# Who makes the small parts: lo parts moved to GpSimd, signs folded into ScalarE's scaling, and the first chunk's k and q turned on TensorE

## The chip, the core and the metric

The kernel runs on one core of a Trainium2 chip. The metric is the time of one execution on the device, in microseconds (us); the median of several runs counts. The engines are named as the profile names them: PE is TensorE (PEld its weight loads), DVE is VectorE, ACT is ScalarE, POOL is GpSimd, SP is SyncE, which only issues DMAs here. Each engine works through a queue of its own in order.

## What is computed

Attention in which a query sees only the keys of its own hash bucket, then a feed-forward block with ELU:

```python
batch, n_heads, seq, head_dim = (4, 8, 768, 64)      # proj: 64 x 6
q_bits = (np.einsum('bhsd,dk->bhsk', q, proj) > 0)   # k_bits in the same way
mask = q_bucket[:, :, :, None] == k_bucket[:, :, None, :]   # buckets: the six bits as a number
scores = np.where(mask, scale * np.matmul(q, k.transpose(0, 1, 3, 2)), -1000000000.0)
attn = softmax(scores)
x = np.matmul(attn, v)            # heads side by side: 3072 tokens x 512
h = x @ w_in                      # w_in: 512 x 2048, float64
g = np.where(h > 0.0, h, np.exp(np.minimum(h, 0.0)) - 1.0)
out = (g @ w_out).astype(np.float32)   # w_out: 2048 x 512, float64
```

## The kernel before

**Two fp16 numbers for one.** Each operand of a matmul is a pair: hi is the scaled value rounded to fp16, lo the rest. ScalarE makes hi (`scaled`, L143), VectorE makes lo (`rest`, L152) as `x * s - hi` in one instruction. Both are helpers, so many different tiles carry these two lines. The table `ENGINES` says which engine takes which kind, before and after all weights are decoded ("A", "V", "G" for ScalarE, VectorE, GpSimd).

**The work in order.** Batch 0 to 3, two chunks each of half the queries; a chunk has four pairs of heads. A pair's k (`prep_k`) and q (`prep_q`) are scaled by a power of two, split (`split`, tiles `natk`, `nat1q`, `nat2q`), turned from tokens on partitions to features on partitions by DMA transposes on SP's queue (L328, L371, L372, tiles `K1`, `O1`, `O2`), and projected: TensorE makes the hash sums, VectorE turns them to plus or minus bits (`bits`, L291), and small DMAs (L295) lay these as further rows under `K2` and `O2`, so that the scores' second matmul adds the mask. The scores (L508) go through VectorE (L520, maximum), ScalarE's exponential (L536), a split into `hl`, a DMA transpose of it (L551) and the product with V (`attend`, L559). V is split once a batch (`prep_v`, `vhl`).

**The weights** arrive as float64. `wload` (L456) brings 512 KB at a time on SP's queue into one of four staging places (three named `U`, one in `W`); `wdecode` makes float32 of it: ScalarE scales the high word (`w_mul`), VectorE shifts (L468), joins the low word (L469) and sets the sign (L479); TensorE sums magnitudes with a matrix of ones (L472) for the common scale (`wscale`, tiles `w0s` and `w1s` for the two matrices). `wsplit` then makes hi and lo of each of the 32 pieces. A piece's pair is written where the piece before it was read: place d takes the pair whose source is place d + 1.

**The feed-forward stream** (`moe_stream`) starts six slots after the first chunk's scores (a slot is one block of 128 queries of one head). `first` multiplies by w_in (L588), takes the exponential (L599, ScalarE), a GpSimd step (L602), a VectorE step (L603), and splits the result; `second` multiplies by w_out (L624). From there on the order of TensorE's queue is fixed by the program's order; elsewhere a scheduler sets each engine's order from dependences and its own estimates. When the steps of a pair's preparation are written is set by lists of slots: `PREP0` for the first chunk's four pairs (load, sums, split, project, counted before the pair's first slot), `VPREP` for V.

Of the kernel before, what the change touches and what calls it, by code (L numbers as in the profile page):

```python
# [7 lines left out]

# [25 lines left out]
PREP0 = (100, 12, 12, 6)  # L34
# [32 lines left out]
def lsh_attention_moe(  # L67
# [210 lines left out]

    def bits(o, ways, w, which):

        t = ps_a.tile([P, 512], F32, tag="av", name="z")[:, :w]
        quads = len(ways[0][1])
        for n, (x, moving) in enumerate(ways):
            for u, mv in enumerate(moving):
                rows = mv.shape[0]
                nc.tensor.matmul(  # L286
                    t[u * QD : (u + 1) * QD], pj["z"][:rows, x, :], mv, start=n == 0, stop=n == len(ways) - 1
                )
# [2 lines left out]
        nc.vector.tensor_scalar(  # L291
            zb[used], t[used], pj["thr"][used, which : which + 1], (MBIT, -MBIT)[which], ALU.is_gt, ALU.mult
        )
        for u in range(quads):
            d = nc.sync.dma_start(o[D : D + 2 * NB, u * w : (u + 1) * w], zb[u * QD : u * QD + 2 * NB])  # L295
        return d
# [3 lines left out]
    def prep_k(b, ps, sts, sgs):  # L300
        def load():
            with after(0, "first") if b == 0 and "first" in ks[0, 0] else nullcontext():
                for p, st, sg_ in zip(ps, sts, sgs):
                    st["kf"] = stg.tile([P, 2 * NC, D], F32, tag="k", name="kst", bufs=2) if sg_.kf is None else sg_.kf
                    nc.sync.dma_start(
                        st["kf"].rearrange("p (h c) d -> p h (c d)", h=2),
                        k[b, 2 * p : 2 * p + 2].rearrange("h (p c) d -> p h (c d)", c=NC),
                    )
# [13 lines left out]
        def split(st, sg_):  # L322
            s, nat = st["ksc"], sg_.k1
            scaled("n_hi", nat[:, :, :D], st["kf"], s)
            rest("n_lo", nat[:, :, D:], st["kf"], s, nat[:, :, :D])
# [2 lines left out]
            st["first"] = nc.sync.dma_start_transpose(st["K1"], flat(nat))  # L328
# [9 lines left out]
    def prep_q(b, c0, nc_, ps, ksts, sts, sgs):  # L338
        def load():
# [25 lines left out]
        def split(st, sg_):  # L365
# [5 lines left out]
            nc.sync.dma_start_transpose(st["O1"], flat(nat1))  # L371
# [88 lines left out]
    def wdecode(i):  # L460
# [6 lines left out]
        scaled("w_mul", d, hi.bitcast(F32), 2.0**-112)  # L467
        nc.vector.tensor_scalar(di, di, 3, None, ALU.logical_shift_left)  # L468
        nc.vector.scalar_tensor_tensor(di, lo, 29, di, ALU.logical_shift_right, ALU.bitwise_or)  # L469
# [2 lines left out]
        nc.tensor.matmul(  # L472
            wst["acc"], ones, d.bitcast(BF16).rearrange("p (n t) -> p n t", t=2)[:, :, 1],
            start=i == o * NSI, stop=i in (NSI - 1, NSI + NSO - 1),
        )
        if i in (NSI - 1, NSI + NSO - 1):
            nc.vector.tensor_reduce(wst["m2"][:, o : o + 1], wst["acc"], axis=AX.X, op=ALU.max)
        if engine("w_sgn") == "V":
            nc.vector.scalar_tensor_tensor(di, hi, -(2**31), di, ALU.bitwise_and, ALU.bitwise_or)  # L479
        else:  # L480
            sign = hi.bitcast(F32)
            nc.scalar.activation(sign, sign, AF.Sign)
            nc.gpsimd.tensor_tensor(d, d, sign, ALU.mult)
# [91 lines left out]
    def moe_stream(chunks):  # L575
# [4 lines left out]
        def first(c, f):  # L580
# [21 lines left out]
            nc.gpsimd.tensor_scalar(e, e, -1.0, 0.0, ALU.add, ALU.min)  # L602
            nc.vector.scalar_tensor_tensor(e, h, c["ch"], e, ALU.mult, ALU.max)  # L603
# [37 lines left out]
        for c in chunks:  # L641
            ch = small.tile([P, 1], F32, tag="ch", name="ch", bufs=2)
            sg = small.tile([P, 1], F32, tag="sgg", name="sgg", bufs=2)
# [316 lines left out]
```

## Time and profile before

| | |
|---|---|
| median of 3 runs (lowest to highest) | 937.68 us (936.27 to 938.84) |
| the profiled execution's own time, and its span | 935.8 us, 934.0 us |
| mean granted TensorE clock | 0.938 |
| instructions | 14523 |
| DMA bytes moved | 138.47 MB, 404586 packets |

The span is cut in stretches in the prediction. A row of a group reads: line, engine, operation, output <- inputs, partitions x elements, count, then busy time in all, mean time of one in ns, and the idle time of that engine just before these instructions with what ended it.

### The profile page before, as it was taken

What the parts mean: (1) busy time and instruction counts of PE and PEld (TensorE: products, weight loads), DVE (VectorE), ACT (ScalarE), POOL (GpSimd) and SP (SyncE); (2) the same over time, 40 slices, a digit from 0 to 9 for tenths busy, and PEclk for the clock granted to TensorE, in tenths of its full rate; (3) what the DMA queues carried; (4) which work ended last, traced back from release to release, by engine and by line L of the source; (5) the groups of instructions that cost most, each with busy time, mean ns of one, the idle gap of its engine ahead of it and who ended that gap; (6) DMA issues with size and microseconds to landing.
All of it is one profiled execution on the core that took longest, in us unless ns stands there. A gap on an engine that the chain in (4) does not pass through costs nothing.

```text
span 934.0 us, 14523 instructions
## 1 busy us (share of the span) xinstructions
PE 816.6 (87%) x4975; PEld 419.9 (45%) x4975; DVE 717.6 (77%) x1524; ACT 690.7 (74%) x1345; POOL 229.1 (25%) x177
## 2 busy tenths in 40 slices
PE   2445545889989999998989999999999999999996
PEld 0112212444545555554544555554455555555553
DVE  6798999888977877688868877888878778774332
ACT  4577886888978777788788777888878778774332
POOL 1000000222223232332323232333232223223432
PEclk9956656899999999999999999999999999999999
DMA  9999798759698677798988767795876767655000
GB/s 268 254 219 228 214 255 180 127 106 200 121 185 166 134 119 136 138 186 154 171 172 155 139 112 144 153 200 94 162 149 126 119 120 152 102 109 91 35 1 35
DMA packets 404586, 138.47 MB, mean 148 GB/s; under 512 B 380960, under 2 KB 398880, under 8 KB 404512
## 3 DMA queue, kind: packets, MB, share of 16 engines
q1 hardware_dynamic: 402432, 131.25, 70.6%
q0 software_dynamic: 1920, 6.29, 2.0%
q8 instruction: 39, 0.64, 0.3%
q14 instruction: 35, 0.29, 0.1%
q10 hardware_dynamic: 160, 0.00, 0.0%
HBM read 35.65 MB, written 6.29 MB: 45 GB/s over the span
## 4 chain that ended last, share of the span: by engine, by line
PE 49%; DVE 19%; DMA 14%; ACT 8%; issue 7%; POOL 2%; SPq 1%; ACTq 0%; POOLq 0%; DVEq 0%
PE o L624 17%; PE h L588 17%; PE s L508 7%; PE av L559 6%; DVE pt L520 4%; DMA K<-natk 4%; DVE hl L152 4%; ACT pt L536 3%; POOL U L602 2%; DMA O<-nat1q 2%; ACT hl L143 2%; DMA W<-in_moe_w_out_dram 2%; DMA out_dram<-W 1%; DVE vhl L152 1%; PE z L286 1%
## 5 line engine op out<-in xcount | busy, mean ns | idle before, releaser
L602 POOL TENSOR_SCALAR U<-U 128x384 f32<-128x384 f32 x128 | 212.9, 1663 | 670.4 <-ACT U L599 669.8
L588 PE MATMUL h<-x,W 128*128 128x384 f16 x1536 | 281.4, 327 | 4.1 <-DVE U L603 3.3
L624 PE MATMUL o<-W,U 128*128 128x512 f16 x1152 | 282.8, 382 | 1.6 <-DVE U L152 0.9
L152 DVE SCALAR_TENSOR_TENSOR hl<-pt,r,hl 128x768 f16<-128x768 f32 x192 | 191.5, 1019 | 20.0 <-ACT hl L143 19.9
L588 PEld LDWEIGHTS <-W 128*128 128x128 f16 x1536 | 147.8, 98 | 116.5 <-issue 15.8
L536 ACT ACTIVATE pt<-pt,nb,sg 128x768 f32<-128x768 f32 x192 | 195.4, 1018 | 2.3
L143 ACT ACTIVATE hl<-pt,r 128x768 f16<-128x768 f32 x192 | 168.4, 925 | 31.3 <-DVE r L546 30.3
L520 DVE TENSOR_SCALAR_CACHE_REDUCE pt<-s 128x768 f32<-128x768 f32 x177 | 167.9, 949 | 17.3 <-PE s L508 16.0
L508 PE MATMUL s<-K,O 128*128 128x384 f16 x708 | 152.7, 340 | 23.4 <-DVE pt L520 22.4
L624 PEld LDWEIGHTS <-U 128*128 128x128 f16 x1152 | 111.5, 98 | 122.9 <-issue 8.8
L603 DVE SCALAR_TENSOR_TENSOR U<-h,ch,U 128x384 f32<-128x384 f32 x128 | 78.4, 612 | 79.8 <-POOL U L602 79.8
L559 PE MATMUL av<-PT,vhl 128*64 128x384 f16 x1152 | 112.5, 347 | 20.3 <-DMA PT<-hl 6.0
L508 PEld LDWEIGHTS <-O 128*128 128x128 f16 (+1 forms) x768 | 75.0, 102 | 119.1 <-issue 48.7
L599 ACT ACTIVATE U<-h,ch 128x384 f32<-128x384 f32 x128 | 73.0, 570 | 59.1 <-PE h L588 58.6
L143 ACT ACTIVATE U<-U,sgg 128x384 f16<-128x384 f32 x128 | 77.3, 605 | 49.9 <-DVE U L603 49.9
L152 DVE SCALAR_TENSOR_TENSOR U<-U,sgg 128x384 f16<-128x384 f32 x128 | 79.1, 619 | 30.9 <-ACT U L143 30.9
L559 PEld LDWEIGHTS <-vhl 128*64 128x64 f16 x1152 | 71.5, 116 | 66.9 <-issue 12.9
L472 PE MATMUL acc<-W,ones 128*128 128x512 bf16 x32 | 16.8, 549 | 32.4 <-DVE W L469 32.4
L533 ACT ACTIVATE nb<-m,sg 128x2 f32<-128x2 f32 x96 | 27.6, 288 | 16.3 <-DVE pt L520 15.8
L536 ACT ACTIVATION_READ_ACCUMULATOR pt<-pt,nb,sg 128x1 f32 x192 | 36.0, 187 | 0.0
L291 DVE TENSOR_SCALAR zb<-z,pjt 64x384 f16<-64x384 f32 (+1 forms) x48 | 29.0, 604 | 1.4 <-PE z L286 1.1
L286 PEld LDWEIGHTS <-pjz 128*32 128x32 f16 (+1 forms) x320 | 9.3, 94 | 43.9 <-issue 29.8
(102 smaller groups left out, 539.2 us busy)
## 6 DMA issues: line engine op xcount, KB each, us to landing
U<-in_moe_w_in_dram SPq DMA_DIRECT2D x12, 512.0 KB
vf<-in_v_dram SPq DMA_DIRECT2D x16, 384.0 KB
U<-in_moe_w_out_dram SPq DMA_DIRECT2D x12, 512.0 KB
out_dram<-W POOLq DMA_DIRECT2D x24, 256.0 KB, 3.4
qst<-in_q_dram SPq DMA_DIRECT2D x30, 192.0 KB
kst<-in_k_dram SPq DMA_DIRECT2D x14, 384.0 KB
PT<-hl SPq DMA_TRANSPOSE x192
W<-in_moe_w_in_dram SPq DMA_DIRECT2D x4, 512.0 KB
```

The lines of the kernel that those rows point to most:

```text
L143: nc.scalar.activation(o, x, AF.Copy, scale=s)
L152: nc.vector.scalar_tensor_tensor(o, x, s, hi, ALU.mult, ALU.subtract)
L291: nc.vector.tensor_scalar(zb[used], t[used], pj["thr"][used, which : which + 1], (MBIT, -MBIT)[which], ALU.is_gt, ALU.mult)
L508: nc.tensor.matmul(s_tile[:, n, :HALF], st[o][:rows, at, :], kst[kk][:rows, j * NC + n * HC : j * NC + (n + 1) * HC, :].rearrange("p a b - ...
L520: top = nc.vector.tensor_scalar(pt.rearrange("p (n e) -> p n e", n=2), s_tile[:, :, :HALF], CLAMP, None, ALU.max, ALU.max, accum_out=duo[0 ...
L536: nc.scalar.activation(pt, pt, AF.Exp, bias=nb[:, n : n + 1], scale=st["sg"][:, 0:1], accum_out=sm[:, n : n + 1])
L559: nc.tensor.matmul(av[j * D : (j + 1) * D], vt[:, j, c, vx, :], PTs[j][:, :, px, c, :], start=n == 0, stop=n == last,)
L588: nc.tensor.matmul(h, WH[:, g * KT + t, wx, fc * P : (fc + 1) * P], c["xs"][t][:, xx, :], start=n == 0, stop=n == 3 * KT - 1,)
L599: nc.scalar.activation(e, h, AF.Exp, scale=c["ch"])
L602: nc.gpsimd.tensor_scalar(e, e, -1.0, 0.0, ALU.add, ALU.min)
L603: nc.vector.scalar_tensor_tensor(e, h, c["ch"], e, ALU.mult, ALU.max)
L624: nc.tensor.matmul(o[t][:, :DO], g16[:, gx, t * P : (t + 1) * P], WH[:, NSI + 1 + f, wx, :], start=f == 0 and i == 0, stop=f == NF - 1 and ...
```

## The change

Six things:

- **Weights' signs.** ScalarE's scaling of the high word becomes a Prelu with a slope that puts the sign where VectorE's two remaining steps want it; the step L479 goes. The scale of a matrix now comes from Gram products of its 128-column blocks (four small matmuls with the piece itself as both operands) in place of one matmul with ones.
- **Lo parts on GpSimd**: those of the weights always, those of V until all weights are decoded (batch 0). There `rest` is two instructions: a scaling in place (L153 of the changed kernel), then a difference (L154).
- **The first chunk's k and q** are turned by TensorE against an identity (`turned_by_pe`, L289), with ScalarE copying the result out of PSUM (L290). Their bits (`bits_beside`) are made on the partitions where they are needed, so that the small DMAs go.
- **The first chunk's steps are written at other slots**: all loads at the start, and sums, split and project of the four pairs at slots -50, 2, 7 and 12.
- **Loads that waited** for the first pair's turning and small DMAs (V's, and the weights' from the sixth on) now stand behind its first load.
- **The ELU** is kept divided by its scale: GpSimd makes `e * up + dn`, VectorE `min(max(h, 0), that)`, with four numbers a chunk instead of two.

The core of the diff:

```diff
-PREP0 = (100, 12, 12, 6)
+PREP0 = (-50, 2, 7, 12)
...
-    "v_lo": ("V", "V"),
-    "w_mul": ("A", "A"),
-    "w_sgn": ("V", "V"),
+    "v_lo": ("G", "V"),
     "w_hi": ("A", "A"),
-    "w_lo": ("V", "V"),
+    "w_lo": ("G", "G"),
...
+    def turned_by_pe(parts):
+        for o, nat in parts:
+            rows, n = o.shape[0], nat.shape[1]
+            for a in range(0, n, 8):
+                z = min(a + 8, n)
+                t = ps_h.tile([P, 512], F32, tag="h", name="turn").bitcast(F16).rearrange("p (n e) -> p n e", e=P)
+                for i in range(a, z):
+                    nc.tensor.transpose(t[:rows, i - a, :], nat[:, i, :rows], ident)
+                nc.scalar.activation(o[:, a:z, :], t[:rows, : z - a, :], AF.Copy)
+
+    def bits_beside(o, ways, which):
+        used = slice(D, D + 2 * NB)
+        for a in range(0, o.shape[1], 512):
+            w = min(512, o.shape[1] - a)
+            t = ps_h.tile([P, 512], F32, tag="h", name="zh")[:, :w]
+            for n, (x, mv) in enumerate(ways):
+                rows = mv.shape[0]
+                nc.tensor.matmul(
+                    t[D : D + QD], pj["z"][:rows, x, :], mv[:, a : a + w], start=n == 0, stop=n == len(ways) - 1
+                )
+            nc.vector.tensor_scalar(
+                o[used, a : a + w], t[used], pj["thr"][used, which : which + 1], (MBIT, -MBIT)[which], ALU.is_gt, ALU.mult
+            )
...
-            st["first"] = nc.sync.dma_start_transpose(st["K1"], flat(nat))
+            if early:
+                turned_by_pe([(st["K1"], nat)])
+                st["first"] = st["load"]
+            else:
+                st["first"] = nc.sync.dma_start_transpose(st["K1"], flat(nat))
...
+            if early:
+                bits_beside(k2, ((0, k1), (1, k1)), 0)
+                st["done"] = st["load"]
+                return
...
-        scaled("w_mul", d, hi.bitcast(F32), 2.0**-112)
+        nc.scalar.activation(d, hi.bitcast(F32), AF.Prelu, scale=2.0**-112, alpha=-(2.0**32))
         nc.vector.tensor_scalar(di, di, 3, None, ALU.logical_shift_left)
         nc.vector.scalar_tensor_tensor(di, lo, 29, di, ALU.logical_shift_right, ALU.bitwise_or)
...
-        nc.tensor.matmul(
-            wst["acc"], ones, d.bitcast(BF16).rearrange("p (n t) -> p n t", t=2)[:, :, 1],
-            start=i == o * NSI, stop=i in (NSI - 1, NSI + NSO - 1),
-        )
+        for u in range(FG):
+            x = top[:, u * P : (u + 1) * P]
+            nc.tensor.matmul(
+                wst["acc"][:, u * P : (u + 1) * P], x, x,
...
-        if engine("w_sgn") == "V":
-            nc.vector.scalar_tensor_tensor(di, hi, -(2**31), di, ALU.bitwise_and, ALU.bitwise_or)
...
-            nc.gpsimd.tensor_scalar(e, e, -1.0, 0.0, ALU.add, ALU.min)
-            nc.vector.scalar_tensor_tensor(e, h, c["ch"], e, ALU.mult, ALU.max)
+            nc.gpsimd.tensor_scalar(e, e, c["up"], c["dn"], ALU.mult, ALU.add)
+            nc.vector.scalar_tensor_tensor(e, h, 0.0, e, ALU.max, ALU.min)
```

The order of the queues shows three places. First GpSimd's queue up to the first ELU step (L602 before, L650 now). Before, only constants stand ahead of it:

```order
L167 MEMSET ones 128x128
L257 MEMSET nat2q 128x6x64
L257 MEMSET W 128x6x64 x2
L225 MEMSET pjz 128x128
L236 MEMSET pjt 32x1 x8
L237 MEMSET pjt 6x1 x8
L602 ISA
L602 TENSOR_SCALAR U<-U 128x384 x18
```

Now its last rows ahead of the first ELU step, and those behind it, are lo parts of weights (`w1s` is the second matrix's scale):

```order
L153 TENSOR_SCALAR W<-W,w1s 128x512
L154 TENSOR_TENSOR W<-W 128x512
L650 TENSOR_SCALAR U<-U,ch 128x384
L153 TENSOR_SCALAR W<-W,w1s 128x512
L154 TENSOR_TENSOR W<-W 128x512
L650 TENSOR_SCALAR U<-U,ch 128x384
```

All 8 lo parts of V's first batch and 28 of the 32 of the weights have come to stand ahead of it, 4 behind it.

Second, ScalarE's queue around the first ELU exponential (L599 before, L647 now; L536 and L584 are attention's exponentials, rows `W<-W,w1s` the hi parts of the second matrix). Before:

```order
L536 ACTIVATE pt_1363,sm_1385<-pt_1363,nb_1383,sg_776 128x768
L536 ACTIVATE pt_1381,sm_1385<-pt_1381,nb_1383,sg_776 128x768
L568 ACTIVATE x16_1354<-av_1317 128x384
L143 ACTIVATE W_94<-W_94,w1s_941 128x512
L545 ACTIVATE r_1399<-sm_1385 128x2
L599 ACTIVATE U_91<-h_1414,ch_1410 128x384
L143 ACTIVATE W_94<-W_94,w1s_941 128x512
```

Now:

```order
L616 ACTIVATE x16_1545<-av_1508 128x384
L581 ACTIVATE nb_1574<-m_1553,sg_1142 128x2
L142 ACTIVATE W_99<-W_99,w1s_1105 128x512
L584 ACTIVATE pt_1554,sm_1576<-pt_1554,nb_1574,sg_1142 128x768
L584 ACTIVATE pt_1572,sm_1576<-pt_1572,nb_1574,sg_1142 128x768
L647 ACTIVATE U_91<-h_1607,ch_1601 128x384
L593 ACTIVATE r_1590<-sm_1576 128x2
```

As many of attention's exponentials (30) stand ahead of it as before, but 28 hi parts of weights instead of 18, and the 16 copies of turned k and q.

Third, SP's queue behind the loads of the first three pairs. Before, the turnings and bits of pair 0 stand between the loads:

```order
L372 DMA_TRANSPOSE O_216<-nat2q 128x6x128
L371 DMA_TRANSPOSE O_215<-nat1q 128x6x128
L328 DMA_TRANSPOSE K_209<-natk 128x12x128
L456 DMA W<-in_moe_w_in_dram 128x1024
L456 DMA U<-in_moe_w_in_dram 128x1024 x3
L305 DMA kst<-in_k_dram 128x2x384
L371 DMA_TRANSPOSE O_321<-W 128x6x128
L295 DMA K_210<-zb 12x384 x4
L391 DMA vf<-in_v_dram 128x2x384 x4
```

Now loads alone:

```order
L438 DMA vf<-in_v_dram 128x2x384 x4
L503 DMA W<-in_moe_w_in_dram 128x1024
L336 DMA kst<-in_k_dram 128x2x384
L385 DMA qst<-in_q_dram 128x2x192 x2
L503 DMA U<-in_moe_w_in_dram 128x1024
L336 DMA kst<-in_k_dram 128x2x384
L503 DMA U<-in_moe_w_in_dram 128x1024 x2
```

V's first batch has moved ahead of all turning, and of the weights' 32 loads the last stands ahead of the eleventh transpose of `hl` (L599 now), where it stood behind the twentieth.

More of the change, by code (lines that the diff above doesn't have):

```diff
@@ L7 @@
 from concourse._compat import with_exitstack
+from concourse.masks import make_identity
 F16 = mybir.dt.float16
@@ L167, in lsh_attention_moe @@
     nc.gpsimd.memset(ones, 1.0)
+    ident = const.tile([P, P], F16, name="ident")
+    make_identity(nc, ident)
     latest = []
@@ L304, in load @@
                     st["kf"] = stg.tile([P, 2 * NC, D], F32, tag="k", name="kst", bufs=2) if sg_.kf is None else sg_.kf
-                    nc.sync.dma_start(
+                    st["load"] = nc.sync.dma_start(
                         st["kf"].rearrange("p (h c) d -> p h (c d)", h=2),
@@ L338, in prep_q @@
     def prep_q(b, c0, nc_, ps, ksts, sts, sgs):
+        early = b == 0 and c0 == 0
         def load():
@@ L471, in wdecode @@
         o = int(i >= NSI)
-        nc.tensor.matmul(
-            wst["acc"], ones, d.bitcast(BF16).rearrange("p (n t) -> p n t", t=2)[:, :, 1],
-            start=i == o * NSI, stop=i in (NSI - 1, NSI + NSO - 1),
-        )
-        if i in (NSI - 1, NSI + NSO - 1):
-            nc.vector.tensor_reduce(wst["m2"][:, o : o + 1], wst["acc"], axis=AX.X, op=ALU.max)
-        if engine("w_sgn") == "V":
[L479 to L483, printed above, removed]
+        top = d.bitcast(BF16).rearrange("p (n t) -> p n t", t=2)[:, :, 1]
+        last = i in (NSI - 1, NSI + NSO - 1)
+        for u in range(FG):
+            x = top[:, u * P : (u + 1) * P]
+            nc.tensor.matmul(
+                wst["acc"][:, u * P : (u + 1) * P], x, x,
+                start=i == o * NSI and u == 0, stop=last and u == FG - 1, skip_group_check=True,
+            )
+        if last:
+            nc.vector.tensor_reduce(wst["m2"][:, o : o + 1], wst["acc"], axis=AX.X, op=ALU.max)
     def wscale(o):
-        wst["ex", o], wst["sc", o] = powers(wst["m2"][:, o : o + 1], 1, 2.0**-17, W_TOP, f"w{o}", const, rows=True)
+        wst["ex", o], wst["sc", o] = powers(wst["m2"][:, o : o + 1], 1, 2.0**-34, W_TOP, f"w{o}", const, squares=True)
         if o == 1:
@@ L641, in moe_stream @@
         for c in chunks:
-            ch = small.tile([P, 1], F32, tag="ch", name="ch", bufs=2)
-            sg = small.tile([P, 1], F32, tag="sgg", name="sgg", bufs=2)
+            cs = small.tile([P, 4], F32, tag="ch", name="ch", bufs=2)
+            ch, sg, up, dn = (cs[:, i : i + 1] for i in range(4))
             vst = vs[c["b"]][0]
@@ L739, in lsh_attention_moe @@
         early = ns[0] < NP
-        lead = [begin[ns[0]] - x for x in (PREP0 if early else PREP)]
+        lead = [-100, *[PREP0[ns[0]]] * 3] if early else [begin[ns[0]] - x for x in PREP]
         split_at = []
         for n in ns:
-            at = begin[n] - (PREP0 if early else PREP)[2]
+            at = lead[2] if early else begin[n] - PREP[2]
             w = 2 * chunks[pairs[n][0]]["nc"]
@@ L768, in lsh_attention_moe @@
             split_at[i] = a
-            z = max(begin[n] - (PREP0 if early else PREP)[3], a)
-            z_last = z + steps[4] - 1
+            z = max(lead[3] if early else begin[n] - PREP[3], a)
+            z_last = z + (0 if early else steps[4] - 1)
             if early:
@@ L774, in lsh_attention_moe @@
             last = {"split": a, "project": z_last}
-            due += [(a, n, 2, lambda s=steps, i=i: s[2](i)), *[(z + x, n, 3 + x, lambda s=steps, i=i, x=x: s[3](x, i)) for x in range(steps[4])]]
+            due += [(a, n, 2, lambda s=steps, i=i: s[2](i)), *[(z + (0 if early else x), n, 3 + x, lambda s=steps, i=i, x=x: s[3](x, i)) for x in range(steps[4])]]
     due.sort(key=lambda x: x[:3])
```

16 lines of the change are left out of this document (13 added, 3 removed).

## The prediction

> **What bounds the kernel now.** I read the busy shares first, then the time cut at the stages, then what the two borders wait for, the groups by line, and the queue rows.
>
> ```profile
> PE 816.6 (87%) x4975; PEld 419.9 (45%) x4975; DVE 717.6 (77%) x1524; ACT 690.7 (74%) x1345; POOL 229.1 (25%) x177
> ```
>
> The shares hide the stages, so the next view cuts the span at the first exponential of attention (44.3 us), the first ELU exponential (173.9) and two later points. A row has the stretch, busy time and instructions per engine, granted clock, DMA share and GB/s.
>
> ```profile
> core 0: us, PE busy (x) PEld busy (x) DVE busy (x) ACT busy (x) POOL busy (x), PEclk, DMA share, GB/s
> 0.00:44.30 44.30, 13.99 (x51) 3.93 (x52) 30.41 (x101) 21.73 (x43) 2.56 (x25) 1.00 0.94 261
> 44.30:173.90 129.60, 72.45 (x337) 31.20 (x336) 119.23 (x266) 101.59 (x197) 0.00 (x0) 0.62 0.91 211
> 173.90:300.00 126.10, 116.14 (x733) 59.59 (x731) 106.73 (x222) 108.37 (x213) 36.61 (x23) 0.96 0.79 154
> 300.00:914.00 614.00, 601.87 (x3799) 319.46 (x3797) 456.80 (x931) 454.59 (x887) 184.66 (x124) 1.00 0.68 129
> 350.00:375.00 25.00, 25.00 (x161) 13.43 (x160) 20.31 (x45) 18.13 (x35) 6.01 (x4) 1.00 0.79 141
> ```
>
> Up to 173.9 us, the opening, VectorE is busiest (119.2 of 129.6 us, 30.4 before that), TensorE works half the time at a clock of 0.62, the DMA engines are at 0.91 and GpSimd does nothing. From 300 us TensorE is full. Between, it ran 733 matmuls in 126.1 us, where 161 per 25 us make 812: 79 are missing, or 12.3 us. So the end moves with the first ELU step and with what of these 12.3 us comes back; an instruction less after 300 us is worth nothing.
>
> ```profile
> 10.25 0.93 ACT L143 ACTIVATE natk<-kst,ks 128x768 f16<-128x768 f32 x1 [0.27 <-DVE ks L199]
> 40.49 0.82 PE L508 MATMUL s<-K,O 76*128 76x384 f16 x2 [0.43 <-DMA O<-zb]
> 44.29 1.03 ACT L536 ACTIVATE pt<-pt,nb,sg 128x768 f32<-128x768 f32 x1
> 173.94 0.58 ACT L599 ACTIVATE U<-h,ch 128x384 f32<-128x384 f32 x1 [0.46 <-PE h L588]
> 174.68 1.49 POOL L602 TENSOR_SCALAR U<-U 128x384 f32<-128x384 f32 x1 [171.20 <-ACT U L599]
> 289.69 0.73 POOL L638 DMA_DIRECT2D out_dram<-W  x1 [2.50 <-ACT nb L533]
> ...
> 97.77 6.61 DMA W<-in_moe_w_out_dram
> 104.40 1.30 ACT W L143 x2
> ```
>
> The first rows are the timeline's: pair 0's keys are scaled at 10.3 us, but its first scores are finished only at 40.5 us, behind the small DMA of q's sign bits. The last two rows are from the chain that ended last: a weight's transfer, for which ScalarE's queue stands still.
>
> **The change, part by part.** These groups give the prices (count, busy, mean ns):
>
> ```profile
> L479 DVE SCALAR_TENSOR_TENSOR W<-U,W 128x512 int32<-128x512 int32 x24 | 16.4, 681 | 0.7 <-PE acc L472 0.7
> L479 DVE SCALAR_TENSOR_TENSOR W<-W 128x512 int32<-128x512 int32 x8 | 5.4, 681 | 0.1
> L152 DVE SCALAR_TENSOR_TENSOR W<-W,w0s 128x512 f16<-128x512 f32 x16 | 11.9, 746 | 0.6 <-ACT W L143 0.5
> L152 DVE SCALAR_TENSOR_TENSOR vhl<-vf,vs,vhl 128x384 f16<-128x384 f32 x32 | 18.7, 615 | 3.3 <-ACT vhl L143 3.3
> L143 ACT ACTIVATE W<-W,w0s 128x512 f16<-128x512 f32 x16 | 11.4, 711 | 2.0 <-DVE W L152 2.0
> L143 ACT ACTIVATE hl<-pt,r 128x768 f16<-128x768 f32 x192 | 168.4, 925 | 31.3 <-DVE r L546 30.3
> L143 ACT ACTIVATE nat1q<-qst,qs 128x384 f16<-128x384 f32 x30 | 18.0, 600 | 1.0 <-DMA O<-nat1q 1.0
> L143 ACT ACTIVATE W<-U 128x512 f32<-128x512 f32 x24 | 15.7, 665 | 14.8 <-DMA U<-in_moe_w_in_dram 8.1 <-DMA U<-in_moe_w_out_dram 6.5
> L568 ACT ACTIVATE x<-av 128x384 f16<-128x384 f32 x32 | 15.3, 478 | 7.1 <-PE av L559 6.9
> L291 DVE TENSOR_SCALAR zb<-z,pjt 64x384 f16<-64x384 f32 (+1 forms) x48 | 29.0, 604 | 1.4 <-PE z L286 1.1
> L520 DVE TENSOR_SCALAR_CACHE_REDUCE pt<-s 128x768 f32<-128x768 f32 x177 | 167.9, 949 | 17.3 <-PE s L508 16.0
> L472 PE MATMUL acc<-W,ones 128*128 128x512 bf16 x32 | 16.8, 549 | 32.4 <-DVE W L469 32.4
> L472 PEld LDWEIGHTS <-ones 128*128 128x128 bf16 x32 | 3.5, 115 | 25.7 <-issue 25.2
> L257 POOL MEMSET nat2q<- 128x384 f16 x1 | 0.4, 423 | 0.0
> ```
>
> Signs: VectorE loses 24 + 8 steps, 21.8 us, all in the opening. ScalarE's scaling becomes a Prelu of the same shape; I take the same time, with +3 us (a tenth of 32 x 0.665, rounded up) as upper end. V's lo parts: batch 0 has 8, at 0.615 us 4.9 us off VectorE; later batches keep theirs. Weights' lo parts: 32 at 0.746 us leave VectorE, 17 before 173.9 us (12.7 us), 15 after (11.2).
>
> Turning on TensorE: each of four pairs gets copies out of PSUM on ScalarE of 1024, 512, 768 and 768 columns. The nearest rows are 478 ns for 384 columns out of PSUM and (925 - 600)/384 = 0.85 ns a column: 1.02 + 0.59 + 0.80 + 0.80 = 3.2 us, four times 12.8 us more on ScalarE. The sign bits become four VectorE steps of 512 columns and one of 256, with (949 - 604)/384 = 0.90 ns a column 0.72 and 0.49 us, 3.4 us a pair in place of 2 x 0.604: +8.6 us over four pairs.
>
> TensorE's own share: 24 turnings of 128 columns a pair, and four Gram products with a weight load each in place of one 512-column product. By 549 ns for 512 columns, and 115 ns a load, that is some 25 us and 11 us more, beside 72 busy of 129.6 us: hidden; without that cover the opening would be longer by up to 36 us.
>
> SP's queue loses three turnings and six small DMAs a pair:
>
> ```profile
> L371 SPq DMA_TRANSPOSE O<-nat1q x30: 1211/1470/2190, 12.3 to 775.7; - x30
> L328 SPq DMA_TRANSPOSE K<-natk x14: 1297/1436/2204, 14.6 to 669.9; - x14
> L295 SPq DMA_DIRECT2D K<-zb x64: 713/722/1614, 22.2 to 716.6; - x64
> ```
>
> Medians (2 x 1.47 + 1.44 + 6 x 0.72 = 8.7 us a pair, 35 us in all). The loads of weights and V, which stood behind them or were held for the first K, now follow one another, and the twelve transfers, 3.1 MB by their shapes, leave DMA engines that move at most 129/0.68 = 190 GB/s in the turning-heavy stretch from 300 us: 17 us of the opening's 160 busy ones.
>
> Sum for the opening. VectorE: 149.6 - 21.8 - 4.9 - 12.7 + 8.6 = 118.8 us. ScalarE: 123.3 + 12.8, and by the order of its queue 28 weights' hi parts stand ahead of the first ELU step where 18 stood, +7.1: 143.2 us. The busiest engine changes from VectorE to ScalarE. VectorE was idle 24.3 us of 173.9; I give ScalarE the same idleness, which makes 167.5 us: **-6.4 us**. The second stage has 10 hi parts (7.1 us) less on ScalarE and 15 lo parts (11.2 us) less on VectorE, the engines that held TensorE back by 12.3 us. How much returns no row shows; the ends are 0 and 12.3, I take half, **-6.2 us**.
>
> GpSimd is what decides. In its queue 8 lo parts of V and 28 of the weights stand ahead of the first ELU step, each a scaling and a difference that waits for it, and ScalarE's next hi part waits for the difference, since it writes where that one reads. What is queued behind on ScalarE are exponentials and hi parts of attention.
>
> ```profile
> L602 POOL TENSOR_SCALAR U<-U x128: 1484/1494/3849, 174.7 to 920.9; 128x384 f32<-128x384 f32 x128
> L152 DVE SCALAR_TENSOR_TENSOR hl<-pt,r,hl x192: 996/1012/1296, 57.4 to 850.2; 128x768 f16<-128x768 f32 x192
> L536 ACT ACTIVATE pt<-pt,nb,sg 128x768 f32<-128x768 f32 x192 | 195.4, 1018 | 2.3
> ```
>
> No 512-column step of GpSimd was run. Scaled by columns the ends are the memset (0.56 us) and the ELU step (1.99), so 1.1 to 4.0 us for the two; neither row is like these steps, and I take the middle, 2.6. The last 21 lo parts are paired on ScalarE with 14 exponentials (14.3 us), 14 hi parts of attention (13.0), their own 21 (14.9) and some 12 us of smaller ones: 54 us, or 2.6 us for each. So at the middle GpSimd just keeps pace, cost **0**; at 4.0 it is 21 x 1.4 = 29 us late. At 1.1 nothing is gained. The Trainium skill (GPSIMD Engine Reference, 3.1, Elementwise) has 4497 ns for a 2048-column two-input step, which I estimate as 1.1 us for 512, and its section 4.1 sends such work to VectorE; no trace here shows it. With 1.99 for the scaling its figure makes 3.1 us, and the sum would be 10 us higher.
>
> Beside it, VectorE's hi-lo step stood at most 1296 - 1012 = 284 ns longer, whichever GpSimd step of 1494 ns ran with it. VectorE has 48 SBUF steps between the weights' scale and the first ELU step: 48 x 0.28 = 14 us at most, and 24 us of slack. The Trainium skill (SBUF — State Buffer, Summary: rules for kernel authors) says that with two SBUF inputs the second to issue fully blocks; the 284 ns do not bear out a block of a GpSimd step's whole length.
>
> The ELU step's product and sum are of the same shape; at the tail two steps are on the path, so anything between +1 and -2 us; I take 0. GpSimd's output DMAs are issued from 289.7 us on and pass none of the new steps.
>
> Together 935.8 - 12.6 = 923.2 us for the profiled execution, which lay 1.9 us under the median of 937.68: **925 us**.
>
> **Rivals.** First, GpSimd becomes the bound: lo parts over 2.6 us hold ScalarE's hi parts, and the first ELU step comes late by 21 times the excess. From 3.2 us the gain is used up (938), at 4.0 it is 954. For it speak the ELU step's 1494 ns and a maximum of 3849; against it that a step that compares need not price a product. Second, transfers hide the relief: with DMA at 0.91 and ScalarE waiting for weights, the opening keeps its length and only the second stage's half returns: 931. Third, the start counts in full: K, q and their bits need no DMA, so the first exponential should come near 29 us (keys scaled at 10.3 to 11.2, their lo part 1.0, 24 turnings 6, copies 3.2, bits 3.4, the scores and two maxima some 4) where it came at 44.3; if all 15 us pass through, and the second stage returns its 12.3, it is 910. Against it: VectorE was 30.4 us busy meanwhile with weights that must be decoded anyway. Fourth, a port block of half a GpSimd step on the 48 VectorE steps, 48 x 0.75 = 36 us: VectorE at 154.8 and the opening at 179.1 with the same idleness: 935.8 + 5.2 - 6.2 + 1.9 = 937. The Trainium skill (SBUF — State Buffer, as above) has the block for a whole step, twice that.
>
> **How the numbers follow.** Forecast (915 to 928) 0.38; transfers hide it 0.14; start in full 0.13; port block 0.05; GpSimd binds 0.30, a little (to 941) 0.09, hard 0.21. Within 0.3% (2.8 us, about what a measurement of this kernel can tell from no change) are parts of the fourth and of the weak first: 0.13. Slower: 0.25. Faster: 0.62. The range leaves out the last tenth on each side: 909 to 947.
>
> **What would show it.** Right: the first exponential of attention before 32 us, the first ELU exponential at 160 to 170, ScalarE busier than VectorE ahead of it, over 760 matmuls in the 126 us behind it. Wrong: GpSimd busy without a gap ahead of its first ELU step and ScalarE's hi parts waiting for GpSimd; or Prelu rows well over 665 ns; or VectorE's hl rows far over 1.3 us; or weights' transfers still at the head of ScalarE's waits.

## The result, and the profile after

The changed kernel takes 926.05 us (median; 924.35 to 927.75) where the kernel before, run beside it, takes 936.97 (936.09 to 938.84): a ratio of 0.9883, 95% interval 0.9865 to 0.9902. Its profiled execution took 925.77 us, with a span of 923.3. The forecast was 925 us, but the two terms that made it were both off, in opposite directions: the opening gained 1.7 us where 6.4 were forecast, the rest of the span 9.0 where 6.2 were.

The page's busy shares after the change:

```profile
PE 823.7 (89%) x5161; PEld 434.4 (47%) x5161; DVE 698.3 (76%) x1490; ACT 696.0 (75%) x1361; POOL 221.9 (24%) x259
```

The span cut at the first exponential of attention and at the first ELU exponential, then 126.1 us as before, then a full stretch:

```profile
core 0: us, PE busy (x) PEld busy (x) DVE busy (x) ACT busy (x) POOL busy (x), PEclk, DMA share, GB/s
0.00:25.07 25.07, 10.82 (x69) 5.99 (x70) 16.46 (x65) 18.91 (x39) 2.99 (x27) 0.99 0.96 333
25.07:172.25 147.18, 86.67 (x506) 42.33 (x505) 130.34 (x264) 119.35 (x227) 83.93 (x72) 0.65 0.80 188
172.25:298.35 126.10, 123.56 (x788) 65.83 (x787) 105.15 (x231) 108.49 (x217) 33.20 (x33) 0.98 0.82 162
350.00:375.00 25.00, 25.00 (x162) 13.46 (x160) 18.86 (x40) 19.11 (x40) 2.78 (x5) 1.00 0.69 133
```

Three things are to be seen. Attention starts 19 us earlier (25.1 against 44.3), and the opening still ends at 172.25, only 1.7 us earlier: the head start was lost again. VectorE is busy for 16.46 + 130.34 = 146.8 us of the opening, where the forecast had 118.8 and the kernel before 149.7. Behind it 788 matmuls stand in 126.1 us where there were 733. From the first ELU exponential to the end of the span it is 923.3 - 172.25 = 751.1 us, against 760.1.

These groups show why VectorE stayed busy, within the opening (0 to 172.25 us) of the changed kernel; columns as before, mean ns behind the comma:

```profile
L151 DVE SCALAR_TENSOR_TENSOR hl<-pt,r,hl 128x768 f16<-128x768 f32 x28 | 32.2, 1185 | 0.3 <-ACT hl L142 0.3
L518 DVE SCALAR_TENSOR_TENSOR W<-U,W 128x512 int32<-128x512 int32 x24 | 18.3, 764 | 0.2
L517 DVE TENSOR_SCALAR W<-W 128x512 int32<-128x512 int32 x32 | 17.0, 540 | 0.9 <-ACT W L516 0.8
L568 DVE TENSOR_SCALAR_CACHE_REDUCE pt<-s 128x768 f32<-128x768 f32 x16 | 15.2, 948 | 0.1
...
L161 DVE COPY nat1q<-nat1q 128x384 f16<-128x384 f16 x6 | 3.8, 640 | 0.0
```

L517 is the shift of a weight's decoding, L518 the join of its low word, and L151 on `hl` the hi-lo step of attention; L568, which reads PSUM, is attention's maximum. In the opening of the kernel before (0 to 173.94 us) they took:

```profile
L152 DVE SCALAR_TENSOR_TENSOR hl<-pt,r,hl 128x768 f16<-128x768 f32 x28 | 27.9, 1011 | 1.1 <-ACT hl L143 1.1
L469 DVE SCALAR_TENSOR_TENSOR W<-U,W 128x512 int32<-128x512 int32 x24 | 16.1, 680 | 0.0
L468 DVE TENSOR_SCALAR W<-W 128x512 int32<-128x512 int32 x32 | 13.3, 419 | 4.3 <-ACT W L143 4.2
```

What goes with the longer steps stands in the timeline of VectorE and, in the second fence, of GpSimd around 96 us (start, length):

```profile
95.61 1.00 DVE L518 SCALAR_TENSOR_TENSOR W<-U,W 128x512 int32<-128x512 int32 x1
96.54 1.90 DVE L151 SCALAR_TENSOR_TENSOR hl<-pt,r,hl 128x768 f16<-128x768 f32 x1
```

```profile
96.16 1.47 POOL L154 TENSOR_TENSOR W<-W 128x512 f16<-128x512 f32 x1
87.25 2.60 POOL L154 TENSOR_TENSOR W<-W 128x512 f16<-128x512 f32 x1
```

VectorE's hi-lo step starts at 96.54 and ends at 98.44, 0.81 us behind the end of GpSimd's difference at 97.63. Of the 1.09 us that both ran it lost 0.89, so it stood for most of the time until GpSimd was done. Nor is GpSimd spared: the difference takes 1.16 us in the median and 2.60 at 87.25, just behind the start of a hi-lo step of VectorE (87.16).

### The profile page after: what moved, and what is told of

Its sections match the earlier page's. It is cut to its first block, busy times and chain, and to the rows that moved or that the text cites. A ratio compares the mean times of both kernels' runs of the same rounds, so it can differ in the third digit from the quotient of the medians.

```text
span 923.3 us, 14935 instructions
## 1 busy us (share of the span) xinstructions
PE 823.7 (89%) x5161; PEld 434.4 (47%) x5161; DVE 698.3 (76%) x1490; ACT 696.0 (75%) x1361; POOL 221.9 (24%) x259
## 4 chain that ended last, share of the span: by engine, by line
PE 45%; DVE 19%; DMA 13%; ACT 12%; issue 8%; POOL 1%; SPq 1%; ACTq 0%; POOLq 0%; DVEq 0%
PE h L636 16%; PE o L672 15%; PE s L556 7%; PE av L607 6%; DVE pt L568 5%; DVE hl L151 4%; DMA K<-natk 4%; ACT pt L584 3%; DMA O<-nat1q 3%; ACT hl L142 3%; DMA PT<-hl 2%; DMA out_dram<-W 2%; DVE W L518 1%; ACT U L647 1%; PE z L315 1%
## 5 line engine op out<-in xcount | busy, mean ns | idle before, releaser
L650 POOL TENSOR_SCALAR U<-U,ch 128x384 f32<-128x384 f32 x128 | 113.4, 886 | 572.1 <-ACT U L647 506.0
L151 DVE SCALAR_TENSOR_TENSOR hl<-pt,r,hl 128x768 f16<-128x768 f32 x192 | 193.9, 1038 | 6.3 <-ACT hl L142 5.9
L584 ACT ACTIVATE pt<-pt,nb,sg 128x768 f32<-128x768 f32 x192 | 195.3, 1018 | 2.2
L142 ACT ACTIVATE hl<-pt,r 128x768 f16<-128x768 f32 x192 | 168.4, 925 | 29.8 <-DVE r L594 27.6
L568 DVE TENSOR_SCALAR_CACHE_REDUCE pt<-s 128x768 f32<-128x768 f32 x177 | 168.0, 949 | 25.1 <-PE s L556 24.4
L556 PE MATMUL s<-K,O 128*128 128x384 f16 x708 | 151.5, 337 | 22.7 <-DVE pt L568 19.8
L651 DVE SCALAR_TENSOR_TENSOR U<-h,U 128x384 f32<-128x384 f32 x128 | 70.8, 553 | 74.8 <-POOL U L650 74.7
L647 ACT ACTIVATE U<-h,ch 128x384 f32<-128x384 f32 x128 | 72.8, 569 | 66.2 <-PE h L636 66.1
L607 PE MATMUL av<-PT,vhl 128*64 128x384 f16 x1152 | 106.9, 332 | 3.8 <-DMA PT<-hl 3.7
L151 DVE SCALAR_TENSOR_TENSOR U<-U,ch 128x384 f16<-128x384 f32 x128 | 79.6, 623 | 39.7 <-ACT U L142 39.4
L142 ACT ACTIVATE U<-U,ch 128x384 f16<-128x384 f32 x128 | 77.2, 605 | 40.8 <-DVE U L651 40.5
L607 PEld LDWEIGHTS <-vhl 128*64 128x64 f16 x1152 | 68.8, 111 | 44.4 <-issue 15.4
L154 POOL TENSOR_TENSOR W<-W 128x512 f16<-128x512 f32 x32 | 43.5, 1363 | 2.2
L584 ACT ACTIVATION_READ_ACCUMULATOR pt<-pt,nb,sg 128x1 f32 x192 | 36.0, 187 | 0.0
L526 PE MATMUL acc<-W 128*128 128x128 bf16 x128 | 17.8, 283 | 19.7 <-DVE W L518 19.2
L556 PE MATMUL so<-K,O 128*128 128x384 f16 (+1 forms) x60 | 18.7, 449 | 17.9 <-DVE pt L568 16.6
```

Source lines behind the costliest of these rows:

```text
L142: nc.scalar.activation(o, x, AF.Copy, scale=s)
L151: nc.vector.scalar_tensor_tensor(o, x, s, hi, ALU.mult, ALU.subtract)
L154: nc.gpsimd.tensor_tensor(o, x, hi, ALU.subtract)
L556: nc.tensor.matmul(s_tile[:, n, :HALF], st[o][:rows, at, :], kst[kk][:rows, j * NC + n * HC : j * NC + (n + 1) * HC, :].rearrange("p a b - ...
L568: top = nc.vector.tensor_scalar(pt.rearrange("p (n e) -> p n e", n=2), s_tile[:, :, :HALF], CLAMP, None, ALU.max, ALU.max, accum_out=duo[0 ...
L584: nc.scalar.activation(pt, pt, AF.Exp, bias=nb[:, n : n + 1], scale=st["sg"][:, 0:1], accum_out=sm[:, n : n + 1])
```

## The experiments

One table first. "Lo" is the lo parts on GpSimd, "sign" ScalarE's signs, "turn" the turning on TensorE with its slots and early loads, "ELU" the new step. Times of events come from the timelines, busy times and matmuls from the cut spans. "Last weight decoded" is the end of VectorE's last decoding step, the join or, where VectorE still sets it, the sign. (The 107 and 155 us in the expectations of x2 and x4 are earlier points of the same decoding.) The last column is the span less the first ELU exponential. Every ratio is to the kernel before, whose median was 936.75 to 937.38 in the four sets of runs.

| kernel | us | ratio (95% interval) | first exponential | last weight decoded | first ELU exponential | VectorE busy ahead of it | matmuls in the 126.1 us behind it | from there to the end |
|---|---|---|---|---|---|---|---|---|
| before | 936.97 | 1 | 44.3 | 162.1 | 173.9 | 149.7 | 733 | 760.1 |
| changed: all four | 926.05 | 0.9883 (0.9865 to 0.9902) | 25.1 | 107.8 | 172.3 | 146.8 | 788 | 751.1 |
| x1: no lo | 921.42 | 0.9835 (0.9818 to 0.9852) | 25.8 | 108.8 | 169.7 | 149.4 | 783 | 749.3 |
| x2: no turn | 943.55 | 1.0073 (1.0057 to 1.0088) | 43.2 | 145.8 | 194.5 | 137.7 | 782 | 748.1 |
| x3: no ELU | 927.49 | 0.9908 (0.9886 to 0.9930) | 26.5 | 112.1 | 169.8 | 144.6 | 744 | 758.9 |
| x4: no sign | 945.03 | 1.0086 (1.0062 to 1.0109) | 26.4 | 150.6 | 185.1 | 167.1 | 736 | 757.8 |
| x5: lo alone | 950.53 | 1.0137 (1.0114 to 1.0160) | 43.4 | 171.7 | 178.8 | 146.8 | 687 | 771.0 |
| x6: sign, ELU | 944.75 | 1.0076 (1.0058 to 1.0094) | 42.0 | 142.4 | 191.0 | 146.1 | 764 | 750.8 |
| x7: turn, ELU | 937.34 | 1.0001 (0.9984 to 1.0018) | 26.9 | 151.1 | 185.0 | 164.3 | 764 | 750.4 |
| x8: ELU alone | 939.02 | 1.0011 (0.9993 to 1.0028) | 43.1 | 160.9 | 172.4 | 149.8 | 716 | 763.7 |
| x9: x6, loads freed | 934.37 | 0.9966 (0.9948 to 0.9983) | 47.6 | 104.5 | 178.4 | 142.8 | 749 | 751.9 |
| x10: no lo for V | 920.73 | 0.9830 (0.9810 to 0.9850) | 25.0 | 110.8 | 170.8 | 144.6 | 788 | 748.0 |
| x11: x1, slots later | 928.48 | 0.9906 (0.9892 to 0.9920) | 25.6 | 106.3 | 177.4 | 150.4 | 786 | 748.8 |
| x12: x1, slots earlier | 930.06 | 0.9916 (0.9895 to 0.9937) | 25.2 | 107.9 | 177.7 | 152.5 | 788 | 750.5 |

### Undoing one part at a time

**x1, lo parts back on VectorE.**

```diff
-    "v_lo": ("G", "V"),
+    "v_lo": ("V", "V"),
...
-    "w_lo": ("G", "G"),
+    "w_lo": ("V", "V"),
```

> The changed kernel with the lo parts of the weights and of V's first batch back on VectorE (the tables' rows v_lo and w_lo all V); the rest of the change stays. Theory A (VectorE paid for GpSimd's work): ahead of the first ELU exponential the changed kernel's VectorE steps are 21.6 us longer in sum than the same steps at the durations of the kernel before, which is about what the 25 moved lo parts had cost VectorE (17.3 us). Then this kernel's shift, join and hl steps go back to 419, 681 and 1011 ns, VectorE's busy time ahead of the first ELU exponential stays within 5 us of the changed kernel's 147 us, and the time is within 3 us of 926. Theory B (the relief of VectorE is real and is what brought the gain): VectorE is 15 us or more busier ahead of the first ELU exponential, which comes at 178 or later, and the time is 932 to 940.

Measured 921.42 us, the first ELU exponential at 169.74. The mechanism is theory A's; its time is 4.6 us below the changed kernel's, better than the 3 us either way that the theory allowed: with 38 lo parts more VectorE is busy only 2.6 us longer ahead of the first ELU exponential. The opening's groups (0 to 169.74 us):

```profile
L151 DVE SCALAR_TENSOR_TENSOR hl<-pt,r,hl 128x768 f16<-128x768 f32 x28 | 27.6, 1010 | 1.1 <-ACT hl L142 1.1
L518 DVE SCALAR_TENSOR_TENSOR W<-U,W 128x512 int32<-128x512 int32 x24 | 16.3, 683 | 0.1
L568 DVE TENSOR_SCALAR_CACHE_REDUCE pt<-s 128x768 f32<-128x768 f32 x16 | 15.2, 950 | 0.1
...
L517 DVE TENSOR_SCALAR W<-W 128x512 int32<-128x512 int32 x32 | 13.2, 418 | 3.3 <-ACT W L516 3.2
L151 DVE SCALAR_TENSOR_TENSOR W<-W,w0s 128x512 f16<-128x512 f32 x16 | 11.9, 745 | 0.0
```

The shift, the join and the hi-lo step are back at their old times. Taken over all groups of the opening (count by difference of the means), the changed kernel's steps are 20.9 us longer than at the durations of x1, and the lo parts that x1 has there cost VectorE 27.2 us (11.9 + 10.4 + 4.9). So moving them saved VectorE some 6 us and not 27, and each lo part then had to pass GpSimd's queue as well. Of the 4.2 us between the two spans (919.1 and 923.3), 2.5 lie in the opening and 1.7 behind it.

**x2, no turning on TensorE** (chunk 0's k and q as in the kernel before, with `PREP0 = (100, 12, 12, 6)` and the loads held for the pairs' turning).

> The changed kernel with the first chunk's k and q turned by DMA and their bits laid by small DMAs, at the slots of the kernel before; signs, lo parts and ELU as changed. Theory A (the turning let the weights come early: the last weight was decoded at 107 us where it was 155, and the second stage runs full because of it): without it the last decode is at 145 or later, the first attention exponential at 40 to 44 us, fewer than 770 matmuls stand in the 126 us behind the first ELU exponential, and the time is 932 to 938. Theory B (the turning only moved the start, which the stretch to 172 us gave back): within 3 us of 926, with the first ELU exponential at 170 to 174 all the same.

Measured 943.55 us: past both theories, and slower than the kernel before, with VectorE 12 us less busy than there. Of theory A's signs the start (43.2) and the last decode (145.8) came, but 782 matmuls and not fewer than 770. The first ELU exponential stands at 194.5. What the runs show of why stands with x6 and x9.

**x3, the old ELU step.**

```diff
-            nc.gpsimd.tensor_scalar(e, e, c["up"], c["dn"], ALU.mult, ALU.add)
-            nc.vector.scalar_tensor_tensor(e, h, 0.0, e, ALU.max, ALU.min)
+            nc.gpsimd.tensor_scalar(e, e, -1.0, 0.0, ALU.add, ALU.min)
+            nc.vector.scalar_tensor_tensor(e, h, c["ch"], e, ALU.mult, ALU.max)
...
```

With it go back the two numbers a chunk of the kernel before, in place of four.

> The changed kernel with the ELU step of the kernel before (GpSimd adds and takes a minimum, VectorE multiplies and takes a maximum). Theory A (the ELU term is nothing but the tail): GpSimd's ELU step is back at 1.49 us, TensorE stays full from 300 us on, and the time is 926 to 929. Theory B (the shorter step frees VectorE's port and GpSimd for the weights' lo parts in the second stage): 930 to 934, with fewer than 790 matmuls in the 126 us behind the first ELU exponential.

Measured 927.49 us, theory A's time; its interval overlaps that of the changed kernel. The profiled execution shows theory B's sign beside it (744 matmuls and not 788 behind the first ELU exponential), but that exponential came 2.5 us earlier. What the step is worth inside the changed kernel is therefore not settled beyond some 3 us.

**x4, the old signs** (`wdecode` and `wscale` as before).

> The changed kernel with the weights' signs set by VectorE's third step (32 steps of 0.68 us, 21.8 us) and the magnitudes summed with a matrix of ones. Theory A (VectorE is full from 25 to 100 us, so what is taken off it there counts): the last decode comes 15 to 20 us later than 107, the first ELU exponential at 180 to 190, and the time is 932 to 942. Theory B (from 100 us on no engine is full and a chain of waits sets the first ELU exponential): VectorE's gaps there (15 us) take most of it, and the time is within 4 us of 926.

Measured 945.03 us, 3 us past theory A: the first ELU exponential at 185.1 lies in its range, but the last decode is 43 us late and not 15 to 20, and the stretch behind is 6.7 us longer too. Without the signs' relief the changed kernel would have lost to the kernel before.

### The parts alone, and in pairs

**x5, lo parts alone; x6, sign and ELU; x7, turn and ELU; x8, ELU alone:** the edits above, put into the kernel before.

> The kernel before with one part of the change: the lo parts of the weights and of V's first batch on GpSimd. Theory P (every GpSimd lo part costs VectorE about what it saves and makes ScalarE's next hi part wait): VectorE's shift steps rise from 419 to 500 ns or more in the mean, its busy time ahead of the first ELU exponential falls by less than 6 us, and the time is 938 to 950. Theory Q (what was measured is only due to how the parts stand together, and here VectorE is relieved): the first ELU exponential at 165 or earlier and the time below 934.

> The kernel before with the signs in ScalarE's scaling and the new ELU step: turning by DMA as before, all lo parts on VectorE. Beside the run without the turning (943.6) it differs by the lo parts alone. Theory P (GpSimd's lo parts are what made that run slow): 934 or less, the first ELU exponential at 172 or earlier where it stood at 194.5. Theory Q (the turning by DMA is what made it slow, and a lo part on GpSimd costs the same 4.6 us as in the changed kernel): 937 to 941, the first ELU exponential at 185 to 192.

> The kernel before with the first chunk turned on TensorE, its slots and its early loads, and the new ELU step; signs and lo parts on VectorE. Beside the run with the old signs (945.0) it differs by the lo parts alone. Theory P (GpSimd's lo parts made that run slow): 934 or less, the first ELU exponential at 176 or earlier where it stood at 185. Theory Q (VectorE full with signs made it slow, the lo parts cost 4.6 us): 938 to 942, the first ELU exponential at 181 to 186.

> The kernel before with the new ELU step alone (product and sum on GpSimd, a maximum and a minimum on VectorE). Theory A (the step is off the path but at the tail): within 2 us of 937, 725 to 745 matmuls in the 126 us behind the first ELU exponential. Theory B (GpSimd's step stands in the round from TensorE's h to the next product, and its 0.83 us less lets TensorE fill the second stage): 760 matmuls or more there, the stretch from the first ELU exponential to the end 5 us or more shorter than 760.1, and the time 929 to 933.

x5 took 950.53 us, half a microsecond past the upper end of theory P, with VectorE's shift at 515 ns and its busy time only 2.9 us lower. Both stretches lost, the opening 4.8 us and the rest 11.0:

```profile
43.44:178.76 135.32, 73.81 (x337) 30.52 (x336) 116.45 (x241) 100.72 (x195) 64.80 (x49) 0.76 0.87 200
178.76:304.86 126.10, 111.54 (x687) 56.76 (x686) 101.78 (x199) 102.03 (x200) 71.59 (x54) 0.97 0.78 151
```

In the second row GpSimd is busy 71.6 us with the last 16 lo parts of weights and the old ELU steps together, and TensorE has 687 matmuls instead of 733.

x7 took 937.34 us against x4's 945.03, with the first ELU exponential at the same place (185.0 and 185.1): nearer to theory Q, but the lo parts cost 7.7 us there, nearly all of it behind the opening (750.4 us from there to the end against 757.8). x6 took 944.75 against x2's 943.55, the same within the intervals: there they cost nothing, and both theories missed the time (the first ELU exponential at 191.0 lies in theory Q's range). So what made x2 slow is not GpSimd, and theory P is wrong for this pair. x8 took 939.02, the same as the kernel before: theory A, with 716 matmuls a little under its range.

Beside an ELU step that alone changes nothing, turn is worth nothing (x7) and sign costs 7 us (x6), while the two together take 15 us off (x1). The chain of waits of x6 shows what stood between two exponentials of attention 24.2 us apart, at 134.57 and 158.77 (pieces under 0.2 us are left out between the rows):

```profile
135.38 5.11 DMA U<-in_moe_w_out_dram
140.51 0.68 ACT W L467
141.21 0.44 DVE W L468
141.67 0.70 DVE W L469
142.42 0.62 PE acc L477 x4
143.07 0.70 DVE wm L482
144.22 4.50 PE av L558 x36
148.73 3.85 DMA PT<-hl
...
157.62 4.13 DMA PT<-hl
```

The last weight's transfer, its decoding, the matrix's scale, and only then TensorE's products with V, for which the next transposes of `hl` waited. The loads of x6, which wait for the pairs' turning as those of x2 do, were late beside the changed kernel's, which follow (first and last start behind the three durations):

```profile
L454 SPq DMA_DIRECT2D U<-in_moe_w_out_dram x12: 327/328/523, 108.4 to 135.4; - x12
...
L503 SPq DMA_DIRECT2D U<-in_moe_w_out_dram x12: 327/328/335, 58.0 to 96.7; - x12
```

Lateness alone does not make x6 and x2 slower than the kernel before, whose same loads run from 96.3 to 149.3 us with the first ELU exponential at 173.9. Why they come out slower than it with the same hold on the loads no run here shows.

**x9, the loads of x6 set free.**

```diff
-W_HEAD = 8
+W_HEAD = 100
-W_FREE = 5
+W_FREE = 100
```

> The kernel before with the new signs and ELU step (the run of 944.75), and beside that only this: the weights' loads no longer wait for the pairs' turning and small DMAs; k and q are still turned by DMA, at the old slots. In the run of 944.75 the loads 18 to 21 were issued at 108 to 110 us, and 19 of 32 pieces were decoded after 110 us. Theory G (the turning is worth its time because it lets the loads go): the last load is issued before 110 us, the last decode stands at 120 or earlier, the first ELU exponential at 178 or earlier, and the time is 934 or less. Theory H (it is the start and the queue time of the turning itself): the first exponential still comes at 42 us or later, and the time stays at 940 to 946.

Measured 934.37 us, 10.4 less than x6. The last load goes out at 95.0 and the last weight is decoded at 104.5, as theory G has it; the first ELU exponential (178.43) and the time miss its bounds by 0.4 each. So of the 23.3 us between x6 and x1 the loads' hold, lifted first, accounts for 10.4; the other 12.9 belong to the turning itself, its start and its slots, which these runs do not part.

**x10, only V's lo parts back on VectorE** (`"v_lo": ("V", "V")`).

> The changed kernel with the lo parts of V's first batch back on VectorE; those of the weights stay on GpSimd. In the changed kernel VectorE's steps between 29 and 47 us, beside these eight, are 6.9 us longer than without GpSimd, and the eight cost VectorE 4.9 us. If the loss of 4.6 us against the kernel with all lo parts on VectorE lies with the weights' parts: 925 to 928, the first ELU exponential at 171 to 174. If it lies with V's, in the stretch where VectorE is full: 920 to 923, the first ELU exponential at 168 to 170.

Measured 920.73 us, with the first ELU exponential at 170.8, 0.8 past the range given for it: the loss against x1 goes with V's eight lo parts, which fall between 29 and 47 us, where VectorE is full. How they cost it is shown only in part: of the 4.5 us between the two spans (918.8 and 923.3) 1.4 lie in the opening and 3.1 behind it, where no lo part of V runs on GpSimd in either kernel. The weights' 32 on GpSimd neither cost nor gain: VectorE's steps are 14.1 us longer there, by the same count as above.

**x11 and x12, the pairs' slots moved**, with all lo parts on VectorE: `PREP0 = (-50, 4, 10, 16)` and `(-50, 0, 4, 9)`.

> The kernel with all lo parts on VectorE (921.4), with pairs 1 to 3 of the first chunk prepared later: slots -50, 4, 10 and 16 in place of -50, 2, 7 and 12. If preparing pairs ahead of their need holds attention back while VectorE is full, exponentials 3 to 12 come earlier and the time is 915 to 919; if VectorE's sum alone sets the first ELU exponential, it stays at 168 to 172 and the time within 3 us of 921; if the preparation then comes too late for the scores, 924 or more.

> The kernel with all lo parts on VectorE (921.4), with pairs 1 to 3 prepared earlier: slots -50, 0, 4 and 9. If VectorE's sum alone sets the first ELU exponential, it stays at 168 to 172 and the time within 3 us of 921; if preparing ahead of need holds attention back, 924 or more; if pairs 1 to 3 were waited for, 915 to 919.

Measured 928.48 and 930.06 us, 7.1 and 8.6 over x1. The opening is 7.7 and 7.9 us longer, with VectorE only 1.0 and 3.1 us busier: VectorE's sum alone does not set the first ELU exponential, and both slot lists gave the 924 or more of the theories that the place of the steps decides, whether later or earlier. In both there are gaps of over 20 us between exponentials (78.5 to 101.4 and 115.9 to 139.0; 81.9 to 102.8 and 103.8 to 126.4).

The versions that beat both kernels are x10 and x1. They were compared with the kernel before, as the changed kernel was, and their intervals lie apart from its own; between the two no difference can be told.

## Why the prediction was right, and where its steps were wrong

**The opening, -6.4 forecast, -1.7 found: the step that failed is VectorE's sum of 118.8 us.** It was 146.8, so VectorE and not ScalarE stayed the busiest engine. Most of the missing 28.0 us is the price of running beside GpSimd. The prediction bounded it at 14 us by the longest hi-lo step of the kernel before (284 ns over its median) and then left it out of the sum as covered by slack. It is 20.9 us: one step took up to 894 ns longer (1904 against 1010), which is also the prediction's own sign of being wrong, a hi-lo row far over 1.3 us. The row that the bound rested on had only a one-input step of GpSimd beside it; none with two inputs had run. The Trainium skill (SBUF — State Buffer, Summary: rules for kernel authors) has it that of a VectorE step with two SBUF inputs and a GpSimd step that reads SBUF the second to issue fully blocks until the first finishes. The hi-lo step of 1.90 us agrees in the main: it ended 0.81 us behind GpSimd's difference, somewhat less than the 1.01 it takes alone. The prediction weighed that rule against the 284 ns and left it to the fourth rival, at 0.05. That rival's price (36 us, VectorE at 154.8) was nearer to the measured 146.8 than the forecast's.

The rest is an error of the sum. It took durations of rows off a busy time, but consecutive rows of one engine overlap at their ends (in the timeline above the join ends at 96.61, the hi-lo step starts at 96.54). Added row by row (count times mean), VectorE's work ahead of the first ELU exponential fell from 175.7 to 166.8 us: 29.8 removed, where the sum has 30.8, and 20.9 of lengthening. Its busy time fell by only 2.9, from 149.7 to 146.8, so some 6 us of what was removed had been overlap. The same holds on ScalarE: by rows it rose by 19.8 us, as forecast, but its busy time by 15.0, to 138.3 where 143.2 had been forecast.

**"The same idleness" for the busiest engine was no rule.** It came near here, but in x2 VectorE is idle for 56.9 us ahead of the first ELU exponential and in x1 for 20.4, where 24.3 had been taken. The opening is a chain through loads, queue order and VectorE, and not the sum of one engine. The first ELU exponential at 172.3 missed the 160 to 170 that the prediction gave as a sign.

**The second stage, -6.2 forecast as half of 12.3, -9.0 found.** The sign to look for, over 760 matmuls, came with 788. The last four hi parts of weights stand behind the first ELU exponential instead of fourteen. In x3 and x4, where the step or the decoding is old, there are 744 and 736; x7, with the old decoding but all lo parts on VectorE, has 764, so the old decoding alone does not make x4's number. That half of the 12.3 would return was a choice between two ends, as the prediction says.

**GpSimd keeps pace: right.** The rows by source line (minimum, median, maximum in ns) of its two lo steps, the scaling for the second matrix, and of the ELU step:

```profile
L153 POOL TENSOR_SCALAR W<-W,w1s x16: 687/698/1659, 115.0 to 188.2; 128x512 f32<-128x512 f32 x16
L154 POOL TENSOR_TENSOR W<-W x32: 1152/1159/3048, 83.2 to 189.0; 128x512 f16<-128x512 f32 x32
L650 POOL TENSOR_SCALAR U<-U,ch x128: 652/666/2766, 172.9 to 910.4; 128x384 f32<-128x384 f32 x128
```

A lo part is 0.70 + 1.16 = 1.86 us in the medians and 2.3 in the means, under the 2.6 taken, and in the opening GpSimd was idle for 52.6 us waiting for ScalarE's hi parts of weights (34.6 of it ahead of the first). ScalarE waited 1.2 us for GpSimd's differences. The waits of the opening (us in total, times, longest):

```profile
POOL W L153 <- ACT W L142: 52.6, 14, 34.6
ACT W L142 <- POOL W L154: 1.2, 4, 0.6
```

So the first rival did not come; what GpSimd cost was what it held up on VectorE, and not its being late. The estimate of 1.1 us by the Trainium skill (GPSIMD Engine Reference, 3.1, Elementwise) for the two-input step agrees with 1.16.

**ScalarE's prices: right.** The sign costs nothing on ScalarE, and the copies come to 12.4 us where 12.8 were forecast:

```profile
L516 ACT ACTIVATE W<-U 128x512 f32<-128x512 f32 x24 | 15.6, 658 | 7.4 <-DMA U<-in_moe_w_in_dram 4.1 <-DMA U<-in_moe_w_out_dram 3.3
L290 ACT ACTIVATE O<-turn 128x768 f16<-128x768 f16 (+1 forms) x8 | 6.3, 793 | 1.0 <-PE turn L289 1.0
L290 ACT ACTIVATE K<-turn 128x1024 f16<-128x1024 f16 (+1 forms) x8 | 6.1, 800 | 1.0 <-PE turn L289 1.0
```

That ScalarE would be busier than VectorE ahead of the first ELU exponential did not come true (138.3 against 146.8 us).

**The start, in the third rival.** The first exponential came at 25.07 us, before its 29; nothing of it reached the end of the opening, as the forecast had it. **Transfers, the second rival:** ScalarE's waits for weights fell from 24.3 to 10.8 us in the whole. The prediction priced 8.7 us a pair of SP's queue and gave it no term in the sum; beside the old turning, the lifting of the hold on the loads was worth 10.4 us by itself (x9 against x6). **The ELU step** at nothing: x8 bears it out, x3 within its interval.

In sum 923.2 us were forecast for the profiled execution and 925.8 measured: the forecast had the opening 4.7 us too short and the rest 2.8 too long, and the part of the time outside the span grew by 0.7. That the total came within 3 us is thus partly luck: two errors of the stages stood against each other, and in the opening VectorE's sum, 28 us short, was hidden by ScalarE's taking its place as the busiest engine.

## What to carry to other kernels

Before moving elementwise work from a full VectorE to GpSimd, price what VectorE's own SBUF steps lose beside it: here 27 us of work moved saved 6, and the time was better with all of it, or with V's part alone, left where it was. Do not add row durations to a busy time, or take them off it, without asking how much of them overlaps. Parts of a change that share one stage are not added up: turning gave nothing, signs cost 7 us, and both together took off 15, with one freeing the weights' loads and the other VectorE; that both held the same stretch is the likely reason, and is not shown apart. A first stage that is a chain through loads and queues is read from its gaps (which wait stands between two exponentials), and not from the busy time of its busiest engine.

## What the runs showed of the hardware

GpSimd's ELU step of 384 columns, in place, takes 0.67 us as a product and a sum with two per-partition numbers and 1.49 as a sum and a minimum with two constants; which of the two differences does it was not tried. VectorE's steps that read PSUM kept their time beside GpSimd (the maximum 948 ns against 950), while those on SBUF alone lengthened: the hi-lo step's longest is 1904 ns in the changed kernel and 1025 in x1, where GpSimd ran only the new ELU steps (1296 in the kernel before, beside the old):

```profile
L151 DVE SCALAR_TENSOR_TENSOR hl<-pt,r,hl x192: 998/1010/1904, 34.8 to 839.0; 128x768 f16<-128x768 f32 x192
...
L151 DVE SCALAR_TENSOR_TENSOR hl<-pt,r,hl x192: 996/1010/1025, 36.9 to 834.7; 128x768 f16<-128x768 f32 x192
```

The first row is of the changed kernel, the second of x1. Steps with one input lengthened too. In the opening the shift went from 418 to 540 ns in the mean, the copy of 384 columns (`nat1q`) from 254 to 640, and even `sg`, one or two columns wide, from 147 to 298.
